# Transposes of a fused retention and projection kernel on 64x64 quarters of TensorE in place of the whole 128x128 array

## The chip, the cores and the metric

One core of one Trainium2 chip. Times are device microseconds of one launch, medians of a few executions with the lowest and highest. The profile is one profiled execution; its span is some 1.8 us shorter than the time of the same execution. Engines in the profile: PE (TensorE's matmuls), PEld (its weight loads), DVE (VectorE), ACT (ScalarE), POOL (GpSimd), SP (SyncE).

## The reference

Retention for 4 batches, 8 heads, 768 steps, head dimension 64, then a gated projection over 3,072 tokens:

```
for t in range(768):
    state = gamma[h] * state + k[:, :, t] (outer) v[:, :, t]
    y[:, :, t] = scale * q[:, :, t] @ state
x = y as 3072 x 512
h = x @ w_in                     # 512 -> 2048
out = (h * cos(h)) @ w_out       # 2048 -> 512
```

The kernel computes retention in chunks of 128 steps: scores inside the chunk, masked, plus a running state. q, k, v come in f32 and are converted to bf16.

## The kernel before

The work is cut into 12 slots; a slot is one chunk of two of the four batches. Projections of four slots' tokens make a group. The kernel's score matmuls take q and k with the head dimension on partitions, so each slot's q and k are transposed: slots 0 to 5 on TensorE through a PSUM bank (PSUM is the memory that matmuls write to) and a copy, slots from 6 on by DMA. This is the transposing code of slots 2 to 5 (16 matmuls of 128x128 a slot, each holding one head of both sequences) and the copy:

```python
def t_mm(p, u, w):                         # slot p, four heads u, w: 0 = q, 1 = k
    if w == 0:
        held["t", p, u] = banks.take()
    tr = held["t", p, u].bitcast(BF16).rearrange("p (w a t) -> p w a t", w=2, a=HP)
    for a in range(HP):
        x = (kb(p) if w else qb(p))
        nc.tensor.transpose(tr[:, w, a, :],
            x[:, u, 2 * a : 2 * a + 2, :] if p < 2 else x[:, :, 4 * u + a, :], ident)

def t_copy(p, u, w, e):                    # e: VectorE or ScalarE
    ...
    copy(e, qkt[p % NB][:, w, ts(u, HP), :], tr[:, w])
```

Everything up to slot 5 is put in order by a planner inside the kernel, a small simulation of the five engines that emits instructions in the order of simulated start times; a table SHIFT moves the ranks of single pieces of work and a table ON fixes engines. Both tables were tuned, for this code. Units of projection ("h" half the tokens, "f" all of a group) fill TensorE between the pieces of retention:

```python
if p in (2, 3):  units = [("h", p, f) for f in range(0, 16, 2)]
elif p == 0:     units = [("h", p, f) for f in range(0, HALF0, 2)]
elif p == 1:     units = [("h", p, f) for f in range(0, HALF0, 2)] + [("f", 0, f) for f in range(HALF0, 16)]
```

From slot 6 on a loop in fixed order follows, where a slot's retention block sits among projections. The retention matmuls of slots from 2 on already use 64x64 quarters of the array.

## Time and profile before

| | before |
|---|---|
| time, median (lowest to highest) of three executions | 208.85 us (208.56 to 209.44) |
| span of the profiled execution | 206.3 us, granted clock 1.00 |
| PE busy | 201.4 us (98%), 2178 matmuls |
| first projection starts | 15.76 us |
| output block of slot 6, the first in the loop, starts | 77.17 us |

```profile
q8 instruction: 17, 0.28, 0.6%
```

The first list says that PE waits 0.2 us in all after the start, for one copy of a transpose. The last line looks like nothing: 17 transfers of 16 KB in 206 us, 0.6% of the DMA engines' time.

### The profile page before, as it was taken

To read this page: it belongs to the slowest core of one execution; us is meant where nothing else is said; L and a number is where in the kernel's file an instruction comes from. 1 tells how busy PE (TensorE), PEld (TensorE's weight loads), DVE (VectorE), ACT (ScalarE), POOL (GpSimd) and SP (SyncE) were. 2 spreads that over 40 slices of the span, in tenths; PEclk is the share of its full clock that TensorE was granted. 3 is DMA by queue.
4 is the path that set the end of the run, shared out by engine and by line. 5 is a ranking of instruction groups with operands and counts; after the bars stand their busy time and mean duration, and the time that the engine had idled before them with its cause. 6 is when DMAs were issued, how large, how long until landed. Compare 5 with 4: busy or idle time off the path is not lost.

```text
span 206.3 us, 5229 instructions
## 1 busy us (share of the span) xinstructions
PE 201.4 (98%) x2178; PEld 108.6 (53%) x2178; DVE 114.2 (55%) x194; ACT 115.2 (56%) x193; POOL 73.8 (36%) x77
## 2 busy tenths in 40 slices
PE   7999999999999999999999999999999999999994
PEld 2558656868945545445445445454444444444442
DVE  5589897866996548338338438448442444444000
ACT  7567886859855357547546546554555553554120
POOL 8969979899973004305207005200000000000000
PEclk9999999999999999999999999999999999999999
DMA  7999999999998976876877675501101101110212
GB/s 121 186 262 210 314 241 312 255 342 276 344 312 150 231 158 175 201 193 171 192 177 144 151 193 142 153 0 56 53 1 51 51 3 51 51 51 0 104 53 102
DMA packets 58600, 32.15 MB, mean 156 GB/s; under 512 B 47696, under 2 KB 53072, under 8 KB 58576
## 3 DMA queue, kind: packets, MB, share of 16 engines
q0 software_dynamic: 14352, 15.47, 33.9%
q1 hardware_dynamic: 44080, 16.28, 31.1%
q8 instruction: 17, 0.28, 0.6%
q10 hardware_dynamic: 144, 0.07, 0.1%
q14 instruction: 7, 0.06, 0.1%
HBM read 27.26 MB, written 6.29 MB: 163 GB/s over the span
## 4 chain that ended last, share of the span: by engine, by line
PE 78%; DMA 10%; POOL 7%; DVE 2%; issue 1%; ACT 1%; POOLq 0%; DVEq 0%
PE bank L635 37%; PE bank L590 27%; DMA vf<-in_v_dram 10%; PE bank L611 4%; PE bank L389 2%; PE bank L480 2%; PE bank L655 2%; DVE gt L619 1%; PE st_ps L508 1%; POOL qf L281 1%; POOL kf L281 1%; PE bank L494 1%; PE bank L361 1%; POOL w_in_sb L300 1%; POOL ks L281 1%
## 5 line engine op out<-in xcount | busy, mean ns | idle before, releaser
L598 ACT ACTIVATE cosb<-bank,halfpi 128x512 bf16<-128x512 f32 x96 | 65.6, 690 | 53.2 <-PE bank L590 48.0
L635 PE MATMUL bank<-w_out_sb,gt 128*128 128x512 bf16 x368 | 90.9, 379 | 0.0
L602 DVE TENSOR_TENSOR gt<-bank,cosb 128x512 bf16<-128x512 f32 x72 | 49.1, 690 | 55.8 <-ACT cosb L598 55.7
L590 PE MATMUL bank<-xt,w_in_sb 128*128 128x512 bf16 x288 | 73.2, 379 | 0.0
L635 PEld LDWEIGHTS <-gt 128*128 128x128 bf16 x368 | 35.5, 98 | 42.3 <-issue 0.2
L590 PEld LDWEIGHTS <-w_in_sb 128*128 128x128 bf16 x288 | 27.6, 98 | 32.3
L324 POOL TENSOR_TENSOR qs<-qf,gq 128x512 bf16<-128x512 f32 x18 | 18.5, 1044 | 43.5 <-PE bank L480 22.6
L408 DVE TENSOR_TENSOR am<-bank,mask 128x512 bf16<-128x512 f32 x40 | 24.8, 682 | 4.2 <-PE bank L389 4.2
L313 ACT COPY ob<-bank 128x512 f32<-128x512 f32 (+1 forms) x24 | 14.0, 582 | 16.0 <-PE bank L635 13.9
L611 PE MATMUL bank<-xt,w_in_sb 128*128 128x256 bf16 x192 | 22.3, 273 | 0.0
L611 PEld LDWEIGHTS <-w_in_sb 128*128 128x128 bf16 x192 | 18.5, 98 | 3.1
L619 DVE TENSOR_TENSOR gt<-bank,cosb 128x512 bf16<-128x512 f32 x24 | 16.0, 686 | 4.7 <-ACT cosb L598 4.6
L313 ACT CAST xt<-bank 128x512 bf16<-128x512 f32 x21 | 11.4, 588 | 10.8 <-PE bank L480 10.1
L313 ACT CAST ks<-kf 128x512 bf16<-128x512 f32 x20 | 11.5, 625 | 2.7 <-DMA kf<-in_k_dram 2.7
L664 PE MATMUL bank<-zero 128*128 128x512 bf16 x34 | 10.5, 442 | 1.1 <-DVE halfpi L680 1.1
L480 PE MATMUL bank<-am,vs 64*64 64x128 bf16 (+1 forms) x320 | 10.3, 206 | 0.1
L336 POOL TENSOR_TENSOR vs<-vf,gk 128x512 bf16<-128x512 f32 x8 | 8.9, 1113 | 3.3 <-PE bank L480 1.5
L331 POOL TENSOR_TENSOR vs<-vf,gk 128x512 bf16<-128x512 f32 x8 | 8.2, 1042 | 5.2 <-DMA vf<-in_v_dram 3.8
L281 POOL DMA_DIRECT2D vf<-in_v_dram x8 | 9.4, 1182 | 1.0 <-DVE vs L336 0.8
L315 DVE CAST stb<-st_ps 128x512 bf16<-128x512 f32 x9 | 6.2, 687 | 3.8 <-PE st_ps L508 3.3
L389 PE MATMUL bank<-qkt 64*64 64x128 bf16 (+1 forms) x320 | 8.0, 206 | 0.3 <-ACT qkt L313 0.2
L313 ACT COPY qkt<-bank 128x512 bf16<-128x512 bf16 x13 | 7.1, 592 | 1.8 <-PE bank L361 1.2
(66 smaller groups left out, 132.7 us busy)
## 6 DMA issues: line engine op xcount, KB each, us to landing
out_dram<-ob SPq DMA_DIRECT2D x23, 256.0 KB, 2.4
vf<-in_v_dram POOLq DMA_DIRECT2D x8, 512.0 KB, 12.0
qf<-in_q_dram POOLq DMA_DIRECT2D x6, 512.0 KB, 12.5
kf<-in_k_dram POOLq DMA_DIRECT2D x6, 512.0 KB, 12.4
w_out_sb<-in_moe_w_out_dram POOLq DMA_DIRECT2D x4, 512.0 KB, 14.1
qf<-in_q_dram SPq DMA_DIRECT2D x4, 512.0 KB, 4.6
w_in_sb<-in_moe_w_in_dram POOLq DMA_DIRECT2D x4, 256.0 KB, 8.7
w_in_sb<-in_moe_w_in_dram POOLq DMA_DIRECT2D x2, 512.0 KB, 10.5
```

The lines of the kernel that those rows point to most:

```text
L281: eng.dma_start(out=t.rearrange("p b h d -> p (b h) d"), in_=src[ds(2 * bp, 2), :, ds(c * C, C), :].rearrange("b h t d -> t (b h) d"))
L313: nc.scalar.copy(out=out, in_=in_)
L324: ENG[e].tensor_tensor(out=qb(p)[:, b], in0=qf[p % PRE][:, b], in1=bc(gq, ORDER[p] % NC), op=ALU.mult)
L389: return nc.tensor.matmul(ap[b][ts(x, 64), a, lo:], lhsT=kt(p % NB, b, h)[:, ts(x, 64)], rhs=qt(p % NB, b, h)[:, lo:], tile_position=(64 * ...
L408: nc.vector.tensor_tensor(out=am[p % 2][b][u], in0=bank.rearrange("p (a t) -> p a t", a=HP), in1=(dec[:, b] if p < 2 else mask[second(p, 0 ...
L480: m = nc.tensor.matmul(held["yp", p][b][ts(j, 64), a, lo:], lhsT=vs[p % NB][ts(r, 64), b, h, :], rhs=am[p % 2][b][h // 4][ts(r, 64), h % 4 ...
L590: nc.tensor.matmul(bank, lhsT=w_in_sb[:, i, ts(f, 128)], rhs=xt[g % 2][:, i, :], start=(i == 0), stop=(i == KIN - 1))
L598: nc.scalar.activation(out=cb, in_=bank, func=AF.Sin, bias=halfpi)
L602: nc.vector.tensor_tensor(out=gt[g % 2][:, f, :], in0=bank, in1=cb, op=ALU.mult)
L611: nc.tensor.matmul(bank[:, ts(e, 256)], lhsT=w_in_sb[:, i, ts(f + e, 128)], rhs=xt[g % 2][:, i, ts(hf, 256)], start=(i == 0 and e == 0), s ...
L619: nc.vector.tensor_tensor(out=gt[g % 2][:, f : f + 2, ts(hf, 256)], in0=bank.rearrange("p (f t) -> p f t", f=2), in1=cb.rearrange("p (f t) ...
L635: nc.tensor.matmul(bank, lhsT=gt[g % 2][:, f, ts(j, 128)], rhs=w_out_sb[:, f, :], start=(f == 0), stop=(f == KOUT - 1))
```

## The change

The intent: a 128x128 transpose of a bf16 tile takes 55.7 ns of TensorE's time in the trace of the kernel before. In the same trace matmuls on different 64x64 tiles overlap: 16 starts take 129 ns at 93.3 us, 8.1 ns each, where one matmul takes some 0.2 us. Four 64x64 transposes, which hold the data of one of 128x128, would take 32 ns at that rate (an estimate from these figures), so the same data should need little more than half the time on the array. Each half of the tokens gets a PSUM bank of its own.

```diff
-SHIFT = {...}   ON = {...}
-HALF0 = 8
+SHIFT = {...}   ON = {...}            # tuned anew; e.g. ON: "rv11" from "A" to "D"
+HALF0 = 4
+def t_quad(p):
+    bk = [banks.take() for r in range(2)]              # one bank for each token half r
+    ...
+    for w in range(2):
+        x = kb(p) if w else qb(p)
+        for h in range(H):
+            for b in range(2):
+                for r in range(2):
+                    nc.tensor.transpose(
+                        tr[r][ts(b, 64), w, h, :], x[ts(r, 64), b, h, :],
+                        ident[ts(r, 64), ts(r, 64)], tile_position=(64 * r, 64 * b))
+def t_out(p, r, w, e):
+    ...
+    copy(e, qkt[p % NB][:, w, :, ts(r, 64)], tr[:, w])
...
-    tq = tk = add("E", 0.45, ... (t_mm(p, u, 0), t_mm(p, u, 1)), ..., [("bank", 1)], (), "full")
+    t = add("E", 0.46, ... t_quad(p), ..., [("bank", 2)], (), "quad")
-kq = {u: [T["eq", p, u], T["ek", p, u]] for u in range(2)}
+kq = {u: [T["e" + x, p, r] for x in "qk" for r in ((u,) if p < 2 else (0, 1))] for u in range(2)}
```

The last line makes the scores of slots 2 and 3 wait for all four copies of their slot in place of two.

## The prediction

The sum below comes to 208.85 - 1.2 + 0 = 207.65 us, with the 1.2 an estimate between 0.94 and 1.6. The 0.89, 0.50, 0.09 and 0.12 us of a slot are read or worked out from the trace of the kernel before. (The 0.027 us in it, by which 64 columns are shorter than 128, is 0.026 there: 219 ns for one 128x128 transpose, 193 for one 64x64 matmul.) The 0.85 us of the first rival is a supposition of mine that no trace has, and so are its 208.9 to 209.7. That the copies would keep their 0.42 us was expected and not shown in advance.

> **What bounds the kernel now.** I read the page's busy shares first, then the table by stretches, the chain that ended last, TensorE's and SyncE's timelines around the transposes, and the DMA landings.
>
> The busy shares and the stretches name the engine:
>
> ```profile
> PE 201.4 (98%) x2178; PEld 108.6 (53%) x2178; DVE 114.2 (55%) x194; ACT 115.2 (56%) x193; POOL 73.8 (36%) x77
> ...
> 15.76:42.30 26.54, 26.32 (x320) 18.61 (x316) 22.51 (x36) 20.70 (x35) 23.92 (x25) 1.00 1.18 269
> 42.30:69.30 27.00, 26.95 (x529) 18.91 (x529) 19.35 (x32) 16.91 (x30) 20.41 (x19) 1.00 1.00 280
> 69.30:199.80 130.50, 130.37 (x1175) 61.94 (x1174) 61.80 (x94) 66.03 (x105) 16.34 (x16) 1.00 0.41 107
> ```
>
> In the stretch rows the second number is PE's busy time. From 15.76 us, where the first real projection starts, PE is idle for 0.22 + 0.05 + 0.13 us in 184 us. Before 15.76, 10.5 of its busy us are idle-filling matmuls on zeros (34 of them). So after 15.76 each us of PE work removed can be a us of the kernel, if inputs are there. Slots 2 to 5 are all transposed between 26.7 and 55.7 us, in this dense part. The chain that ended last has DMA, GpSimd and VectorE up to 42 us and PE from there, two of the four transposing blocks included:
>
> ```profile
> 23.77 12.89 DMA vf<-in_v_dram
> ...
> 41.67 0.59 ACT qkt L313
> 42.31 0.63 PE bank L389 x26
> ...
> 46.98 1.00 PE bank L361 x16
> ...
> 54.97 0.89 PE bank L361 x16
> ```
>
> This says that two limits lie near each other in the first 70 us: PE work and the stream of loads. That decides how much of a PE saving can be kept (third rival).
>
> PE's timeline shows a transposing block alone (26.68 to 27.58), one behind a block of 64x64 quarters (46.91), a block of quarters alone (57.52), and quarters at 64 columns (32.55):
>
> ```profile
> 26.68 0.39 PE L361 MATMUL bank<-ident,qs 128*128 128x128 bf16 x4
> 26.91 0.39 PE L361 MATMUL bank<-ident,ks 128*128 128x128 bf16 x4
> 27.13 0.39 PE L361 MATMUL bank<-ident,qs 128*128 128x128 bf16 x4
> 27.35 0.39 PE L361 MATMUL bank<-ident,ks 128*128 128x128 bf16 x4
> 27.58 1.03 PE L590 MATMUL bank<-xt,w_in_sb 128*128 128x512 bf16 x4
> ...
> 32.55 0.29 PE L508 MATMUL st_ps<-vs,ks 64*64 64x64 bf16 x8
> ...
> 46.57 0.41 PE L480 MATMUL bank<-am,vs 64*64 64x128 bf16 x16
> 46.91 0.40 PE L361 MATMUL bank<-ident,qs 128*128 128x128 bf16 x4
> ...
> 56.57 1.03 PE L635 MATMUL bank<-w_out_sb,gt 128*128 128x512 bf16 x4
> 57.52 0.64 PE L389 MATMUL bank<-qkt 64*64 64x128 bf16 x32
> 58.09 0.39 PE L635 MATMUL bank<-w_out_sb,gt 128*128 128x512 bf16 x1
> ```
>
> The second number of a row runs from the first start to the last modelled end, so rates come from starts. A slot's 16 transposes go from 26.68 to 27.58, 0.89 us, or 55.7 ns each. The eight 64-column matmuls at 32.55 use two quarters (both columns of one row group): 0.29 less the 0.193 us of one is 0.097 us for three steps, so 32 ns a step in one quarter. A switch in: four 512-column matmuls at 0.216 us from 56.57 end at 57.43, the quarters start at 57.52, 0.09 us later. A switch out: the last quarter starts at 57.52 + 0.64 - 0.216 = 57.94, the next full matmul 0.148 us later instead of 0.056: 0.09 again.
>
> [...] The copies of transposes take 0.416 us on VectorE against 0.68 for f32 sources of the same size[...].
>
> **The change part by part.** For each of slots 2 to 5:
>
> Removed: 16 full transposes, 16 x 55.7 = 0.89 us of PE.
>
> Added: 2 (q, k) x 8 heads x 2 sequences x 2 token halves = 64 transposes of 64x64, 16 in each quarter. The first step of a quarter is longer (57.53 to 57.58, about 53 ns, in single rows of the trace), then 14 steps of 32 ns: 0.053 + 0.448 = 0.50 us from first to last start. That needs a start each 8 ns over four quarters. The output block at 93.3 us has 16 starts in 129 ns, 8.1 ns each, so the rate has been seen. After the last start the exit costs some 0.12 us to the next full matmul: the 0.148 above, less the 0.027 us by which 64 columns are shorter than 128.
>
> Alone between full-size work: 0.09 in + 0.50 + 0.12 = 0.71 in place of 0.89: 0.18 us saved. Behind other quarter work, where today's block pays the leaving (0.148 at 46.76 to 46.91) and then 0.89 = 1.04, the new one has 0.50 + 0.12 + 0.01 = 0.63: 0.40 saved. The halved array time (0.89 to 0.50) is thus eaten to a good part by two mode changes, unless blocks are neighbours.
>
> Sum: in today's places (slots 2, 3 and 5 alone, slot 4 behind the output block of slot 3) 3 x 0.18 + 0.40 = 0.94 us. If the new order of work puts every block next to quarter work: 4 x 0.40 = 1.6 us. The order is planned anew (the ranks and the engine choices of the diff) and the planner counts a mode change, so I take 1.2 us, somewhat under the middle of the two.
>
> Moved: evacuations are the same 16 copies of 128x512 bf16 (0.59 us on ScalarE, 0.42 on VectorE), now by token half. Score matmuls of slots 2 and 3 wait for all four copies rather than two. Today both score units already run together (x32 at 28.61 and 42.31), after the last copy, so nothing is lost; the two later copies can start about 0.2 us sooner because all transposes are done by 0.50 rather than 0.89 us. Two banks are taken at a time rather than one then one; seven are in use, and the trace shows no wait for a bank.
>
> HALF0 from 8 to 4 turns 4 half-width units (0.874 us each, 64 matmuls in 6.99 us) into 4 full-width ones (0.865): 0.04 us. PE should then show 2178 - 64 + 256 - 16 = 2354 matmuls, if the filling ones stay 34. Moves of single conversions between GpSimd, ScalarE and VectorE (36 to 56% busy) are worth nothing directly.
>
> **Rivals.**
> First, that quarters run slower than 32 ns for transposes[...]. Then 64 pairs take 0.85 us and, with the two mode changes, the change is level or loses 0.2 us a slot: 208.9 to 209.7. Against it: 8.1 ns seen at 93.3 us with real matmuls and loads of the same 64x64 shape. For it: no transposes by quarters are in this trace.
>
> Second, that copies become dearer[...]: 16 copies, those on VectorE from 0.42 to 0.68 us. VectorE is at 72 to 85% in the two stretches to 69 us, and the copies stand right before the score matmuls (the 0.22 us wait at 42.09 is for one). Up to 0.26 us for some slots: 208 to 208.6. I give it little.
>
> Third, that the saving turns into a wait for loads. The software queue's landings are evenly spaced, 1.52 us for each half MB of q, k or v, and the last k of slot 7 lands at 60.98 whatever PE does. The DMA transposes of slot 6 come after it:
>
> ```profile
> 62.71 1.34 SPq L350 DMA_TRANSPOSE qkt<-ks  x1
> 64.23 3.03 SPq L350 DMA_TRANSPOSE qkt<-qs  x2
> ```
>
> The output block of slot 5 (from 67.56) has the scores of slot 6 in it, and PE stands still in it from 67.94 to 68.19: data arriving just in time, I think. But today's first transpose starts 1.7 us after that landing, since SyncE's queue holds the tell-tale of slot 4's block (61.65) ahead of it. That one is earlier when PE is earlier. So there is room for about 1.7 us, a little more than the saving. If the room is not there, half the saving is lost: 208.2.
>
> In the other direction, the new order could recover the 0.22 and 0.25 us waits and start the projections a few tenths sooner than 15.76 (its weights land at 15.20): 206.9 to 207.3.
>
> **Time, range, chances.** 208.85 - 1.2 + 0 for the order of work, which I can't read beyond this (gaps recovered against a new wait, both a few tenths): 207.65 us, 0.6% less. Low end: 1.6 saved and 0.45 recovered, 206.8. High end: 0.5 kept less noise (the runs before spread 0.9 us): 208.7. Faster by over 2% would need 4.2 us, more than all 3.6 us that the transposes of these slots take on PE: 0.03. Slower by over 2% needs a badly broken order of work, with 4 us of new PE waits, from a planner that was right to some tenths so far: 0.03. Within: 0.94.
>
> **What would show each step right or wrong.** A transposing group of 64x64, 256 matmuls, with starts of one slot spanning 0.50 us; 32 ns between starts in a quarter (0.5 us or less: right; 0.8: first rival). The change in PE's busy time from 15.8 us to the loop's start 1 to 1.5 us down, and that start 1.2 us earlier than 69.3. Copies into the transposed tile at 0.59 and 0.42 us (0.68: second rival). No PE wait over 0.3 us in the output block of slot 5, and the first DMA transpose about a us earlier than 62.71 (else third rival). From the loop's start to the end: 137 us as now. If that part changes, or if the start of the projections moves by over 0.5 us, the time was made elsewhere than I say.

## More of the kernel before

The prediction shows the busy shares, the stretches, the chain and the timelines. Two views more are of use. First, every wait of PE's matmuls that the profile of the kernel before shows (us in total, times, longest); next, from the page's list of DMA queues, the queue that brings instructions (transfers, MB, share of 16 engines' span).

```profile
PE bank L664 <- DVE halfpi L680: 1.1, 1, 1.1
PE bank L361 <- DMA kx<-in_k_dram: 0.4, 1, 0.4
PE bank L389 <- ACT qkt L313: 0.2, 1, 0.2
```

## The result, and the profile after

| | before | after |
|---|---|---|
| time, median (lowest to highest) | 208.96 us (208.56 to 209.44) | 212.25 us (211.21 to 212.38) |
| ratio | | 1.0146 (95%: 1.0107 to 1.0185) |
| span of the profiled execution | 206.3 us | 209.4 us |
| first projection | 15.76 us | 16.27 us |
| output block of slot 6 | 77.17 us | 80.34 us |
| from there to the end | 129.1 us | 129.1 us |

(The kernel before has a fourth execution here, hence the other median.) A ratio is the mean time of one kernel's fast runs over that of the other's of the same rounds, so it is not quite the ratio of the medians quoted. Executions over 1.5% slower than the fastest of the same kernel are left out of the means. The kernel became slower, within 2%, and outside the predicted range.

From the page of the kernel after, the busy line and the instruction queue:

```profile
PE 202.0 (96%) x2354; PEld 106.1 (51%) x2354; DVE 115.3 (55%) x198; ACT 113.6 (54%) x189; POOL 73.3 (35%) x77
...
q8 instruction: 18, 0.29, 0.6%
```

2354 matmuls, as predicted: 176 more pairs of weight load and matmul, 352 more instructions. The stretches (the second number is PE's busy time, further on the granted clock, the DMA share and GB/s) say where PE now idles:

```profile
16.27:40.00 23.73, 23.46 (x324) 14.57 (x320) 20.51 (x35) 18.00 (x30) 19.76 (x21) 1.00 1.17 270
40.00:60.00 20.00, 17.41 (x428) 12.08 (x426) 15.21 (x28) 11.60 (x21) 19.49 (x19) 1.00 1.08 319
60.00:72.40 12.40, 12.40 (x278) 7.78 (x275) 6.70 (x11) 6.60 (x12) 3.84 (x4) 1.00 0.57 133
```

2.59 us of idle time lie between 40 and 60 us. PE's waits and the chain name them, and what they name is no data:

```profile
PE bank L411 <- issue: 1.6, 1, 1.6
...
PE bank L411 <- ACT qkt L313: 0.5, 2, 0.2
PE bank L516 <- issue: 0.4, 1, 0.4
PE bank L633 <- issue: 0.3, 1, 0.3
```

```profile
51.53 1.07 issue
```

"issue" is time in which the engine waited for nothing that the profile shows. The timeline of the longest, with all engines:

```profile
49.62 0.59 ACT L313 COPY qkt<-bank 128x512 bf16<-128x512 bf16 x1
...
50.05 0.41 DVE L315 COPY qkt<-bank 128x512 bf16<-128x512 bf16 x1
...
50.80 0.24 PE L411 MATMUL bank<-qkt 64*64 64x128 bf16 x1
...
52.60 0.60 PE L411 MATMUL bank<-qkt 64*64 64x128 bf16 x31 [1.57 <-issue]
```

The copies that feed these scores had ended at 50.46. One of the 32 score matmuls ran, and 31 matmuls of the same unit, with the same inputs and banks, started 1.8 us later. A wait for data would have stopped the first. The other two stops are like it, inside a block of slot 3 and inside a projection unit:

```profile
46.41 0.24 PE L516 MATMUL bank<-qkt,stb 64*64 64x128 bf16 x2 [0.40 <-issue]
```

```profile
58.24 0.27 PE L633 MATMUL bank<-xt,w_in_sb 128*128 128x256 bf16 x1
58.80 0.93 PE L633 MATMUL bank<-xt,w_in_sb 128*128 128x256 bf16 x7 [0.28 <-issue]
```

Counting PE's records (a weight load and a matmul are two, and two of its sequencer come first), PE resumes after these stops with instructions 1218, 1474 and 1730: 256 apart, to the instruction. The instruction queue moved 18 transfers of 16 KB for 4708 weight loads and matmuls, 262 for each, and 17 for 4356 before, 256 for each; so I take one transfer to bring 256 instructions, an estimate from these counts, and call them a block. And I take it that PE was out of instructions; the experiments below test it. The trace has the transfers' own times. For each block of 256: when its first instruction runs, when the first packet of the transfer after that starts, when the transfer ends, when the first instruction of the next block runs, and how long that is after the transfer's end (us; the stop is the distance between starts less the usual step of such matmuls, 0.06 us or 0.11):

```
kernel   block starts  transfer        next block  after transfer's end  stop
after    40.39         44.06 to 45.11  46.41       1.30                  0.56
after    46.41         50.19 to 51.15  52.60       1.45                  1.75
after    52.60         56.38 to 57.35  58.80       1.45                  0.45
after    58.80         59.99 to 61.55  65.76       4.21                  none
before   32.62         36.44 to 37.48  43.11       5.63                  none
before   43.11         46.28 to 47.33  49.67       2.34                  none
before   49.67         52.72 to 53.78  61.69       7.91                  none
```

In all rows but the fourth, where the loads are nearly over, the first packet comes 3.0 to 3.8 us after the block is entered; the transfer takes 1.0 us, and at a stop PE goes on 1.3 to 1.45 us after it. So the three blocks of the changed kernel that end in a stop took 6.0 to 6.2 us, however few us their work needs. In the kernel before the densest block of this stage takes 6.56 us, and its successor's transfer is 0.9 us earlier than it would be at a stop. (The starts are those on the array, and I take them for the time at which a block was entered only right after a stop. In the loop of projections, packets start up to 5.1 us ahead of the counted place: in the kernel before, at 158.45 for a block that starts at 163.59. At 0.216 us a pair that is some 47 instructions, an estimate of how far the fetch was ahead of the array there. So a block behind wide matmuls had its successor's transfer earlier.)

Now the transposes themselves. PE's timeline of slot 2, and the copies by engine (lowest, median and highest ns of one, then from when to when):

```profile
28.11 0.45 PE L383 MATMUL bank<-ident,qs 64*64 64x64 bf16 x32
28.39 0.46 PE L383 MATMUL bank<-ident,ks 64*64 64x64 bf16 x32
28.78 1.04 PE L612 MATMUL bank<-xt,w_in_sb 128*128 128x512 bf16 x4
30.06 0.63 PE L411 MATMUL bank<-qkt 64*64 64x128 bf16 x32 [0.24 <-ACT qkt L313]
```

```profile
L315 DVE COPY qkt<-bank x14: 404/416/425, 5.3 to 58.8; 128x512 bf16<-128x512 bf16 x14
L313 ACT COPY qkt<-bank x10: 567/585/592, 6.6 to 57.5; 128x512 bf16<-128x512 bf16 x10
```

From the first transpose to the next projection are 28.78 - 28.11 = 0.67 us, in place of 0.89; the change from full matmuls to quarters before them (a mode change, below) costs 0.09 (six matmuls of 512 columns from 26.72, at 0.216 us each, end at 28.02). In slots 2 to 5 the whole is 0.73 to 0.76 us, so about 0.14 us is saved a slot. The copies kept their pace: medians of 416 ns on VectorE and 585 on ScalarE, 415 and 591 before.

The profiles' difference of 3.1 us then closes. Before the first projection: +0.51. From there to slot 6: 64.07 us in place of 61.41, +2.66. It is made of the three stops, 0.56 + 1.75 + 0.45 = +2.76; the transposes, 4 x 0.14 = -0.57; waits of slot 2's and slot 3's scores for the last copy, twice 0.31 by the distance of starts in place of once 0.29, +0.33; one wait of 0.18 at 32.54 for w_out; HALF0, -0.04. The sum is +2.66. That it closes so well is partly luck, as the small terms are uncertain by some hundredths. PE's busy time from the first projection to the loop's start (69.30 us before, 72.40 after) is 53.27 us in both: the profile counts some 0.17 us of a matmul's modelled end as busy before each stop, and that hides most of what the transposes saved.

### The profile page after: what moved, and what is told of

Its sections match the earlier page's. It is cut to its first block, busy times and chain, and to the rows that moved or that the text cites. A ratio compares the mean times of both kernels' runs of the same rounds, so it can differ in the third digit from the quotient of the medians.

```text
span 209.4 us, 5571 instructions
## 1 busy us (share of the span) xinstructions
PE 202.0 (96%) x2354; PEld 106.1 (51%) x2354; DVE 115.3 (55%) x198; ACT 113.6 (54%) x189; POOL 73.3 (35%) x77
## 4 chain that ended last, share of the span: by engine, by line
PE 89%; DVE 3%; ACT 3%; DMA 1%; issue 1%; DVEq 0%; POOLq 0%; SPq 0%; ACTq 0%
PE bank L657 37%; PE bank L612 29%; PE bank L633 8%; PE bank L686 3%; PE bank L411 2%; PE bank L502 2%; PE bank L677 2%; PE st_ps L530 2%; ACT cosb L620 1%; DMA qf<-in_q_dram 1%; PE bank L516 1%; ACT qkt L313 1%; PE bank L361 1%; PE bank L383 1%; DVE gt L624 1%
## 5 line engine op out<-in xcount | busy, mean ns | idle before, releaser
L612 PE MATMUL bank<-xt,w_in_sb 128*128 128x512 bf16 x304 | 76.5, 379 | 0.0
L612 PEld LDWEIGHTS <-w_in_sb 128*128 128x128 bf16 x304 | 29.1, 98 | 34.4
L633 PE MATMUL bank<-xt,w_in_sb 128*128 128x256 bf16 x160 | 19.0, 273 | 0.3 <-issue 0.3
L633 PEld LDWEIGHTS <-w_in_sb 128*128 128x128 bf16 x160 | 15.3, 98 | 3.3 <-issue 0.5
L686 PE MATMUL bank<-zero 128*128 128x512 bf16 x34 | 11.1, 458 | 1.1 <-DVE halfpi L702 1.1
L411 PEld LDWEIGHTS <-qkt 64*64 64x64 bf16 x320 | 6.8, 107 | 3.7 <-issue 1.7
```

The lines of the kernel that those rows point to most:

```text
L411: return nc.tensor.matmul(ap[b][ts(x, 64), a, lo:], lhsT=kt(p % NB, b, h)[:, ts(x, 64)], rhs=qt(p % NB, b, h)[:, lo:], tile_position=(64 * ...
L612: nc.tensor.matmul(bank, lhsT=w_in_sb[:, i, ts(f, 128)], rhs=xt[g % 2][:, i, :], start=(i == 0), stop=(i == KIN - 1))
L633: nc.tensor.matmul(bank[:, ts(e, 256)], lhsT=w_in_sb[:, i, ts(f + e, 128)], rhs=xt[g % 2][:, i, ts(hf, 256)], start=(i == 0 and e == 0), s ...
L686: nc.tensor.matmul(bank[:, : 256 * n].rearrange("p (n t) -> p n t", n=n), lhsT=zero[:, :128], rhs=zero.unsqueeze(1).to_broadcast([128, n, ...
```

## The experiments

Theory F (fetch): the 64 quarter transposes of a slot are 128 instructions in place of 32, these use up blocks faster than the instruction queue can bring them while the loads are running, and TensorE stops at ends of blocks. Rivals: the new order of work is worse (the diff replaces both tables); the quarters cost more than their array time in another way, through mode changes, banks or copies; or the stops are waits for data that the profile doesn't attribute. Most runs move one of these at a time. All runs gave right results unless said. "Before" is the kernel before on the same chip in the same rounds. Medians are of all executions, ratios of the fast ones; only quads_old_plan has slow ones, two of four. Chips differ between the jobs, so runs of different jobs are compared by their ratios.

| run | this, us | before, us | ratio (95%) |
|---|---|---|---|
| plan_only | 212.53 | 209.36 | 1.0171 (1.0123 to 1.0220) |
| quads_old_plan | 214.05 | 209.36 | 1.0152 (1.0082 to 1.0223) |
| row_halves | 209.52 | 209.36 | 1.0015 (0.9994 to 1.0036) |
| shifted | 210.40 | 209.36 | 1.0050 (1.0024 to 1.0075) |
| full_new_order | 208.95 | 209.11 | 0.9986 (0.9965 to 1.0008) |
| before_cut | 211.97 | 209.11 | 1.0136 (1.0108 to 1.0163) |
| light_loads | 215.03 | 209.11 | 1.0281 (1.0234 to 1.0328) |
| row_halves_rv | 210.07 | 209.11 | 1.0041 (1.0016 to 1.0065) |
| light_heads | 211.84 | 208.96 | 1.0140 (1.0108 to 1.0172) |
| after_again | 211.46 | 208.96 | 1.0117 (1.0098 to 1.0137) |
| best_full | 208.42 | 208.96 | 0.9971 (0.9949 to 0.9993) |
| best_row | 208.70 | 208.96 | 0.9980 (0.9965 to 0.9995) |

### The diff's two halves, each alone

plan_only: the transposes of before, with the new tables and HALF0.

```diff
-SHIFT = {before}  ON = {before}  HALF0 = 8
+SHIFT = {after}   ON = {after}   HALF0 = 4
```

> The new ranks, engine choices and HALF0 with the old 128x128 transposes. Theory F (PE runs into the end of its fetched instructions, which come in blocks of 256 and take about 6.2 us from one block's start to the next block's being there while loads run): 192 pairs of instructions fewer, so no PE stop over 0.3 us without a releaser between 40 and 60 us; left are the start of projections 0.5 us later and the full transposes, 209.2 to 210, ratio to before 1.00 to 1.005. Rival P (the new order of work is itself the worse one): the stops stay, 211 to 212.5, ratio 1.01 to 1.017.

212.53 us: theory F was missed by far, and if this were all, the order would carry the whole loss. But the planner simulates anew with the costs of the old transposes, so the order that came out is neither kernel's. The output block of slot 5 follows that of slot 4 directly, with nothing left to fill the time, and PE waits for data there:

```profile
PE bank L480 <- DVE am L408: 0.9, 2, 0.5
PE bank L431 <- DVE gt L315: 0.6, 1, 0.6
PE st_ps L508 <- DVE stb L315: 0.5, 1, 0.5
```

Its first projection is late too (17.11 us). One of its four executions (213.97 us) had a lower granted clock, 0.992. No stop lies at an end of a block. So the run tells nothing of the order that the changed kernel has; full_new_order below does.

quads_old_plan: the other half, the new transposes with the old tables.

```diff
-SHIFT = {after}   ON = {after}   HALF0 = 4
+SHIFT = {before}  ON = {before}  HALF0 = 8
```

> The 64x64 transposes with the old ranks, engine choices and HALF0. Theory F: the stops without a releaser come back in some form, since the instructions are as many: 210 to 212, ratio 1.005 to 1.015, with PE stopping at instructions that are a multiple of 256 apart. Rival P: at most 208.6, ratio 0.995 to 1.0, no such stop.

214.05 us median (211.22 to 215.16), with a ratio of its fast runs of 1.0152, just above the ratio that F gave; only two runs are fast (211.22 and 213.64). The profiled execution was a slow one (215.16 us, clock 0.984), so I read from it only the place of its stop, inside the transposes of slot 4:

```profile
48.59 0.41 PE L383 MATMUL bank<-ident,ks 64*64 64x64 bf16 x29
52.42 0.27 PE L383 MATMUL bank<-ident,ks 64*64 64x64 bf16 x3 [3.42 <-issue]
```

The transposes after it have the operands of the 29 before it, and PE resumes with instruction 1474. So the quarters bring stop and loss without the new tables too. But here again the planner simulates anew, so the order is neither kernel's, and the size of the loss isn't that of the quarters alone.

### The number of instructions

row_halves: the changed kernel with 32 transposes a slot in place of 64. Each takes 64 tokens of both sequences in a 64x128 tile; banks, copies, order and mode changes stay.

```diff
-for b in range(2):
-    for r in range(2):
-        nc.tensor.transpose(tr[r][ts(b, 64), w, h, :], x[ts(r, 64), b, h, :],
-            ident[ts(r, 64), ts(r, 64)], tile_position=(64 * r, 64 * b))
+for r in range(2):
+    nc.tensor.transpose(tr[r][:, w, h, :], x[ts(r, 64), :, h, :],
+        ident[ts(r, 64), ts(r, 64)], tile_position=(64 * r, 0))
```

> The changed kernel in all but the tile of its transposes: 64x128 (a token half by two sequences' 64 columns), 32 a slot in place of 64. PE time of a slot's transposes the same 0.51 us from first to last start (two row halves, 32 ns a step), half of the added instructions gone. Theory F: stops of 2.8 us shrink to under 0.6 us in all; 209 to 210, ratio 1.0 to 1.006. Rival P, and a rival in which waits for data or banks stop PE: as the changed kernel, 211 to 212.5, ratio 1.01 to 1.017.

209.52 us. One stop at an end of a block is left, again at instruction 1218, now between transposes of slot 4:

```profile
48.14 0.38 PE L382 MATMUL bank<-ident,qs 64*128 64x64 bf16 x13
48.75 0.21 PE L382 MATMUL bank<-ident,qs 64*128 64x64 bf16 x3 [0.23 <-issue]
```

Its transfer ended at 47.44, 1.31 us before. Starts of a slot span 0.45 us, even less than with quarters. As banks, layout of the copies and mode changes are those of the changed kernel, they are not what costs 3 us.

shifted: the changed kernel with 68 more instructions ahead of everything: each of the 34 filling matmuls on zeros cut in two. No data and no order changes; only the places where blocks end.

```diff
-nc.tensor.matmul(bank[:, : 256 * n]..., lhsT=zero[:, :128], rhs=zero (n times 256 columns), ...)
+for i in range(n):
+    nc.tensor.matmul(bank[:, ts(i, 256)], lhsT=zero[:, :128], rhs=zero, ...)
```

> The changed kernel with its 34 idle-filling matmuls of 512 columns before 16 us each cut into two of 256: the same PE time, 68 PE instructions more before everything that counts. Theory F: stops at the same counts of PE instructions (1218, 1474, 1730 or other multiples of 256 from them), so 68 instructions earlier in the program than in the changed kernel; sizes change, time 210.5 to 212.5. Rival D (they wait for data or a bank): the stops stay before the same matmuls as in the changed kernel, in the output block of slot 3 and before the second score matmul of slot 4, with 0.6 and 1.8 us.

210.40 us, a little under the range that F gave. The stops at 1218 and 1730 are gone, the one at 1474 is there; but that count now falls into the transposes of slot 4, and the scores where it was go through without a stop:

```profile
48.54 0.26 PE L383 MATMUL bank<-ident,ks 64*64 64x64 bf16 x11
50.35 0.35 PE L383 MATMUL bank<-ident,ks 64*64 64x64 bf16 x21 [1.54 <-issue]
...
52.48 0.63 PE L411 MATMUL bank<-qkt 64*64 64x128 bf16 x32
```

The stop moved with the count of instructions, not with the data. This rules out the rival of hidden data waits. It is also 0.7 to 1% cheaper than the changed kernel with nothing but the phase of the blocks changed. One correction to the 6.0 us comes from it: the block that ends in this stop was entered at 45.98, right behind wide matmuls, its successor's transfer ran from 48.01 to 48.95, and PE went on at 50.35, after 4.4 us. So the 6 us are no constant. What is alike in the stops of all runs is the last part, 1.40 us after the transfer's end here and 1.2 to 1.6 us elsewhere.

before_cut: the converse. The kernel before, with its own order and full transposes, gets more instructions that do the same work: first-group output matmuls of 512 columns cut into four, the half-width projections of slots 2 and 3 into two. 320 pairs more, for some 0.7 us of array time, an estimate from the steps in the trace of the kernel before (216 ns for 512 columns and 109 for 256, against four or two of 55.7 for 128).

```diff
-nc.tensor.matmul(bank, lhsT=gt[...][:, f, ts(j, 128)], rhs=w_out_sb[:, f, :], ...)
+for x in range(4):                        # group 0 only
+    nc.tensor.matmul(bank[:, ts(x, 128)], lhsT=gt[...][:, f, ts(j, 128)],
+                     rhs=w_out_sb[:, f, ts(x, 128)], ...)
...                                        # and 256 columns into 2 x 128 for slots 2 and 3
```

> The kernel before, its transposes and order untouched; the output matmuls of the first group cut into four of 128 columns and the half-width projections of slots 2 and 3 into two of 128: 320 pairs more, the array time only 0.7 us more (64 x 7 ns + 128 x 2 ns). Theory F: stopping at a multiple of 256 PE instructions, a round trip of 6.1 us laid over the trace of the kernel before gives 2.0 to 2.4 us of stops between 33 and 52 us: 211.3 to 212.5, ratio 1.011 to 1.016. If instruction count does not matter: 209.9 to 210.4, ratio 1.002 to 1.005, no such stop.

211.97 us, in the range that F gave. No quarter transposes, no mode change more than before, old tables; and the stop is there, in the middle of a projection whose inputs are long in place:

```profile
48.58 1.78 PE L613 MATMUL bank<-xt,w_in_sb 128*128 128x128 bf16 x29
52.12 2.06 PE L613 MATMUL bank<-xt,w_in_sb 128*128 128x128 bf16 x34 [1.76 <-issue]
```

Its transfer ended at 50.82, 1.3 us earlier. A second one of 0.46 us is at 68.24.

### The order of work

full_new_order: the changed kernel with its order kept instruction for instruction (the planner still sees one piece of 0.46 us with two banks), but 16 full transposes in that piece.

```diff
-for b ..., for r ...: nc.tensor.transpose(tr[r][ts(b, 64), w, h, :], ..., tile_position=...)
+nc.tensor.transpose(tr[h // HP][:, w, h % HP, :], x[:, :, h, :], ident)
...
-copy(e, qkt[p % NB][:, w, :, ts(r, 64)], tr[:, w])
+copy(e, qkt[p % NB][:, w, ts(r, HP), :], tr[:, w])
```

> The changed kernel's order of work kept instruction by instruction, but each slot's 64 quarter transposes replaced by 16 full ones into the same two banks (heads 0 to 3 and 4 to 7). Theory F (fetched instructions run out): 192 pairs fewer, no PE stop of over 0.4 us between 44 and 62 us; PE pays 4 x (0.89 - 0.75) = 0.56 us more than the row halves did: 209.6 to 210.4, ratio 1.002 to 1.006. Rival P (the new order is the loss): as the changed kernel, ratio 1.01 to 1.017.

208.95 us, below what F gave, and no stop at the end of a block. The densest block takes only 5.0 us, and yet its successor's transfer is 2.38 us ahead, for it began 1.6 us after the block was entered. Apart from waits before 13 us and three gaps of 0.16 us where the record of a matmul is missing (2139 matmuls, 2162 weight loads), the list of waits holds only the late start:

```profile
PE bank L449 <- DVE gt L315: 0.5, 1, 0.5
```

So the new order is as good as the old one, and what stands between this kernel and the changed one is the quarters alone: 1.0146 / 0.9986 = 1.016, some 3.3 us (by the ratio of the second job, 1.0117, some 2.7 us).

### What makes a transfer late

light_loads and light_heads give wrong results (relative errors 0.57 and 0.56). They load half of the data for late slots, to see if the instruction transfers come sooner when less is ahead of them. light_loads drops half of the partitions of slots 5 to 7:

```diff
-out=t.rearrange("p b h d -> p (b h) d"), in_=src[ds(2 * bp, 2), :, ds(c * C, C), :]...
+out=t.rearrange("p b h d -> p (b h) d")[:64], in_=src[ds(2 * bp, 2), :, ds(c * C, 64), :]...
```

> Wrong result on purpose: the changed kernel with half of the bytes of q5, v5, v6, q7, k7 and v7 not loaded, so that less stands ahead of an instruction fetch after 47 us; PE's program is the same to the instruction. Theory F with the fetch queued behind the loads: from a block's start to its fetch's first packet 3.7 us becomes 2.5 or less for fetches after 48 us; the stop at instruction 1474 falls from 1.75 to under 1.0 us and the one at 1730 goes; the one at 1218 stays. 210 to 211.5, ratio 1.004 to 1.01. If the fetch time does not depend on the loads: the stops as in the changed kernel, ratio 1.013 to 1.017.

215.03 us, the wrong way: slower. The first packet of an instruction transfer came up to 5.1 us after the block's start, and there were three stops. By my reading of its trace the loads landed no earlier than the changed kernel's. So it was not shown that half the bytes in this shape is a lighter load; the run is no test of what it was to test.

light_heads drops whole heads of some loads instead, so all partitions stay (q and v of slot 5, v of slot 6, q, k and v of slot 7):

```diff
-out=t.rearrange("p b h d -> p (b h) d"), in_=src[ds(2 * bp, 2), ...]
+out=t[:, 0], in_=src[2 * bp, ...]           # for the loads named
```

> Wrong result on purpose, as light_loads but with half of the heads instead of half of the partitions left out (light_loads moved fewer bytes at no higher speed: its loads landed no earlier). The changed kernel's PE program to the instruction. Theory F with the fetch queued behind the loads: these six loads take about 0.8 us each in place of 1.5, the fetches after 48 us start 2.8 us or less after their block's start in place of 3.7, the stop at 1474 falls below 1.2 us and the one at 1730 goes; the stop at 1218, before the lighter loads, stays at 0.3 to 0.7 us. 210 to 211.3, ratio 1.004 to 1.011. If the fetch time does not depend on the loads: stops and time as in the changed kernel.

211.84 us. Partly a miss: the stop at 1474 stayed, 2.0 us; its transfer (51.12) came right behind the landing of a piece of w_out (51.07), which is not lightened. The transfer after it, for the block entered at 53.65, came after 2.0 us in place of 3.8, ended at 56.67, and the stop at 1730 was gone. So the load traffic has a part in the delay: one transfer, seen once. The whole gained nothing over the changed kernel of the same job (after_again, 211.28 to 211.82 us). Two losses show in the profiled execution: its projections wait 0.48 us for w_in at 18.04, and the granted clock was 0.50 from 54.70 to 58.10, after the stop. But it is the slowest of the four (213.29 us, clock 0.992); the other three had clocks of 0.999 to 1.0 and took 211.21 to 212.11, so the clock explains that one alone. Its stretches, with the granted clock third from the end:

```profile
53.60:54.70 1.10, 1.05 (x34) 0.73 (x34) 0.41 (x1) 0.00 (x0) 1.10 (x2) 1.00 1.07 358
54.70:58.10 3.40, 3.40 (x16) 2.14 (x15) 2.12 (x5) 0.69 (x1) 3.40 (x4) 0.50 0.51 169
58.10:62.00 3.90, 3.85 (x90) 2.93 (x90) 3.03 (x6) 2.47 (x4) 2.14 (x3) 1.00 0.02 4
```

For these 3.4 us the granted clock was half of that around it. A lower clock was also seen after the 2.0 us stop of light_loads (mean of the execution 0.992), and in quads_old_plan for 6.83 us from 51.34 on, within its 3.4 us stop (0.50 from 52.40 to 58.00, mean 0.984); not after the 1.75 us stop of the changed kernel, nor after 1.92 us in before_cut (both with a mean of 1.000). In light_heads the execution so lost more than its stop; that the stop is the cause of the lower clock was not tested.

after_again repeats the changed kernel beside light_heads, unedited.

> The changed kernel once more beside the others: 211.5 to 212.5, ratio 1.012 to 1.017; stops of PE without a releaser at instructions 1218, 1474 and 1730 and nowhere else over 0.3 us after 20 us, each 6.0 to 6.3 us after the block before it was entered.

211.46 us, just under the expected range, with stops of 0.52, 1.75 and 0.45 us at 46.42, 52.62 and 58.81: the same three instructions.

### Mending the start, and the best version

In row_halves and full_new_order the first projection starts at 17.0 to 17.2 us. The new tables had moved a conversion of slot 1 (the second half of its raw v, "rv11") from ScalarE to VectorE, and the second half of slot 1's output waits for it. (The changed kernel has this wait too, of 0.20 us in its profile and 0.41 in after_again, where the first projections start at 16.27 and 16.52.) row_halves_rv puts it back:

```diff
-ON = {..., "rv11": "D", ...}
+ON = {..., "rv11": "A", ...}
```

> The row halves (64x128 transposes, 32 a slot), with the conversion of slot 1's second raw v back on ScalarE, where the kernel before had it. If that move is what delays the first projections, they start 0.6 us or more earlier than in the row halves (17.16 us, beside loads that land alike) and the time falls by as much: 208.6 to 209.0, ratio 0.996 to 0.999. If something else delays them: 209.5 as the row halves.

The start came back (16.24 in place of 17.16 us) and the time did not: 210.07 us, 0.5 us worse than row_halves. The last transfer of the kernel, issued by ScalarE, took 1.41 us to issue. ScalarE's timeline at the end of row_halves_rv, then of row_halves:

```profile
204.14 1.41 ACTq L680 DMA_DIRECT2D out_dram<-ob  x1
```

```profile
204.80 0.37 ACTq L680 DMA_DIRECT2D out_dram<-ob  x1
```

ScalarE now has 191 instructions that the page counts in place of 189 (the 176 and 175 of an expectation below are on no page), and a transfer of 8 KB on an instruction queue, q14, lies at 203.88 to 204.38. In the traces the last such transfer comes when ScalarE has started 318 to 320 of its records (318 in the kernel before, at 193.97; 319 in the changed one, at 208.34); the last DMA issue is its record 318 in row_halves, just ahead of that, and 320 here. My reading is that it had fallen into a block that wasn't there yet. best_row is this kernel with the last transfer issued by SyncE; best_full is full_new_order with both moves.

```diff
-(nc.sync, nc.scalar)[i].dma_start(out=..., in_=...)
+nc.sync.dma_start(out=..., in_=...)
```

> The same two moves with the row halves: from row_halves (209.5) the start's 0.8 us off: 208.5 to 209.0, ratio 0.996 to 0.999; one stop of 0.4 us stays in slot 4's transposes. If ScalarE's fetch at the end was not what cost row_halves_rv its time: 209.7 or more.

> Full transposes in the new order, the second raw v of slot 1 on ScalarE, and the last output DMA issued by SyncE, so that ScalarE has 175 instructions as before (with 176, in row_halves_rv, its last DMA issue took 1.41 us in place of 0.37 beside a fetch of 8 KB). First projections at 16.2 us in place of 17.0, no long issue at the end: 208.95 - 0.7 = 208.0 to 208.5, ratio 0.994 to 0.998.

208.70 us and 208.42 us, both as expected; the one move is worth 1.3 us in the row form by the ratios (1.0041 to 0.9980, in two jobs). That SyncE is no faster by itself shows at the end of the profiles: from the last copy's end to the end of the span are 3.37 us in best_row, 3.36 in row_halves and 4.40 in row_halves_rv. best_full has ratio 0.9971 to before, with an interval up to 0.9993: the best kernel here is 0.3% faster than before, hardly more than the noise and not to be told from best_row, and has no part of the change's transposes, only its order with the two moves.

## Why the prediction was wrong

The step that failed is "Added: 2 (q, k) x 8 heads x 2 sequences x 2 token halves = 64 transposes of 64x64": it priced these 64 matmuls by their time on the array alone. Their instructions were taken as free. The stops at ends of blocks cost 2.76 us in the profile, where the step saved 0.57; row_halves, shifted, before_cut and full_new_order show that these stops come with the number and place of the instructions, and not with data, banks, copies, mode changes or the order. It could have been seen: 17 transfers of 16 KB, and a block of 256 instructions that took 6.56 us in a stage where transfers began 3 us after a block's start; that is hindsight. No wait of the kernel before pointed there: its list of PE's waits has three entries, and none is "issue".

By its other steps:

- Array time: right. Starts of a slot span 0.51 to 0.55 us, 0.50 predicted, so the 8.1 ns a start of the other matmuls nearly holds for transposes (8.2 to 8.7) and the first rival is out.
- Saving: 0.14 us a slot where 0.18 was predicted for a block alone. All four blocks stand alone between full-size work, so the 0.40 beside other quarters was never earned: 0.57 us of the 1.2 in the sum. The sign that the prediction named, 1 to 1.5 us less of PE's busy time up to the loop, did not come (53.27 us in both), and the loop starts at 72.40 us in place of 69.30.
- Copies: 0.59 and 0.42 us as before; the second rival is out. But "nothing is lost" by waiting for all four was wrong: slots 2 and 3 wait 0.24 us each by the profile.
- Third rival: not met, and hardly tested, as PE came later and not earlier. PE stands still in slot 5's block from 71.16 to 71.36, shorter than before; as the prediction thought, it is data arriving just in time, for PE goes on 0.05 us after the first DMA transpose landed (71.31; before, 0.04 after 68.15). That DMA transpose came at 65.98 in place of 62.71, later only because PE was later.
- "+0 for the order of work": the start moved by +0.51 us in the profile, just over the half us at which the prediction said that time was made elsewhere. The rest of the new order is a small gain (60.86 us from the first projection to slot 6 in full_new_order, 61.41 before).
- From slot 6, and from the loop's start, to the end: unchanged, as predicted (129.1 and 137.0 us).

Open: that a transfer starts on entering the block before is inferred from times, mostly 3 to 4 us after the entry under loads, but 2.0 us in shifted and 1.6 us in full_new_order; nothing in the trace shows the request, and what sets the delay is only in part shown (one lighter transfer). Why the changed kernel lost 1.5% in one job and 1.2% in the other isn't known. Whether quarters would pay if instructions were saved elsewhere, or the blocks lay better, wasn't tried.

## What to carry to other kernels

Cutting a matmul into parallel tiles saved array time here (0.14 us a slot) and spent instructions (96 more a slot), so count both: find the densest 256 PE instructions of the stage, as the stops here were 256 apart, and compare their time with what the instruction transfers take there (here 6.0 to 6.2 us a block at the three stops under loads, that is about 21 pairs of weight load and matmul in a us). This is a warning and no threshold: blocks of 5.0 us in full_new_order and 5.6 us in the changed kernel (28.20 to 33.77) went without a stop, as the transfers began early enough. A stop that the profile puts down to "issue", in the middle of a unit whose first matmul ran, is a suspect; count instructions between two such stops, and shift them by some idle ones to see whether the stop follows the count. And, by my reading of row_halves_rv, one conversion more pushed an engine's last instruction over the same edge (1.41 us for the issue in place of 0.37), so a small move should be judged by the whole time.
